# Attention steps of 20 queries in three slots instead of two, and the two weight copies of a step declared independent

## The chip, the cores and the metric

The kernel runs on one core of a Trainium2 chip. The metric is the device time of one execution in microseconds. Three runs of the kernel before took 1334.59, 1334.84 and 1337.12 us (median 1334.84).

## The reference

Three layers follow each other: an attention over 4 batches, 12 heads, 448 positions and 64 features, whose scores are mixed across heads before the softmax and whose weights are mixed across heads after it; a two-layer network with a sigmoid gate; and a mixture of 8 experts. The change touches the attention alone:

```python
scores = scale * np.matmul(q, k.transpose(0, 1, 3, 2))
scores = np.einsum('bhij,hg->bgij', scores, w_pre)
scores = scores - np.max(scores, axis=-1, keepdims=True)
attn = np.exp(scores)
attn = attn / (np.sum(attn, axis=-1, keepdims=True) + 1e-09)
attn = np.einsum('bhij,hg->bgij', attn, w_post)
return np.matmul(attn, v).astype(np.float32)
```

## The kernel before, in words

The 448 queries of a batch are cut into tiles of 120, 120, 120 and 88, so there are 16 tiles. A tile's raw scores are computed on TensorE for pairs of heads (`qk`, L89), scaled and moved out of PSUM by ScalarE and VectorE (`qk_ev`, L94 and L95), and stored to a DRAM tile `S` (L96). Tiles are cut into steps of 20 queries (the last step of an 88 tile has 8), 92 steps in all. A step's scores come back from DRAM in another layout (`relay`, L104 and L106): one partition holds one query and one head, 60 partitions hold 5 queries by 12 heads, a "unit" is 10 queries (two groups `c` of 5), and a step has two units `a` (one in the 8-query step).

For a step, `premix` (L112) mixes the heads with a block-diagonal matrix into PSUM, `maxi` (L116, VectorE) takes the negative row maximum, and `exp` (L119, ScalarE) writes the exponential E and its row sum. `weights` (L122, L123 on VectorE, L126 on GpSimd) takes the reciprocal of the sum and multiplies the second mixing matrix with it: the result is the tile M, one per unit, so that the division is part of the second mixing. `post` (L135) multiplies pieces of E with M on TensorE: 32 small matmuls per unit, whose results, already transposed, go to the PSUM tile `psa` (one buffer of two banks, one bank per group `c`, 240 columns per unit). `post_ev` copies them into the tile AT, which holds the transposed weights of a whole query tile: unit 0 by ScalarE (L142), unit 1 by VectorE (L143), each reading both banks. `av` (L151) multiplies AT with the values for two heads at a time, six times per tile, and `av_ev` (L155, L156) moves each half of a tile's result out and stores it.

The order on every engine is the order in which the program issues the instructions; no scheduler changes it. The loop over slots `s` sets it: slot s issues the relay of step s+3, Q, K and V loads, `premix`, `maxi` and `exp` of step s, `post` and `post_ev` of step s-1, the `av` calls due in this slot, the `qk` calls due (new scores for a later tile, one call per slot as a rule), `weights` of step s, and last `qk_ev`. A step thus spans two slots. All stores and loads are issued on SP in this order.

From slot 88 on, every slot also calls `beside` twice. Each call issues the next entries of the list EARLY, which belong to the second stage: loads and decodes of its packed weights (L246 on ScalarE, L251 to L254 on VectorE), splits of a float32 tile into a rounded part and a remainder (L227, L228, L259, L260 on ScalarE, VectorE and GpSimd), and the first matmuls (L268). The first of three L268 groups issued there comes in slot 92, the second in slot 93, the third in slot 95. Behind the last slot the second stage opens its remaining memory, issues two more weight loads and goes on with its own loop, in which every step decodes two weight tiles on VectorE.

The wait of VectorE's copy for ScalarE's copy comes from the framework, which orders instructions that write overlapping address ranges of one tile; the two copies of a step write interleaved columns of AT. `declare_no_dep` tells it that two instructions do not depend on each other.

Of the kernel before, what the change touches and what calls it, by code (L numbers as in the profile page):

```python
# [6 lines left out]
F32 = mybir.dt.float32  # L7
# [10 lines left out]
TI = 120  # L18
DM, FF, E = 768, 2048, 8
# [18 lines left out]
def attention(tc, qT, kT, vT, w_pre, w_post, x_out, beside=None):  # L38


    nc=tc.nc
    tiles=[(b,i0,min(TI,S-i0)) for b in range(B) for i0 in range(0,S,TI)]
    steps=[]; first={}
# [4 lines left out]
    units=lambda s: range((steps[s][2]+9)//10)  # L48
# [11 lines left out]
    def load_mix():  # L60
# [3 lines left out]
        for c in range(2):  # L64
# [2 lines left out]
            sel(out=x,in_=x,pattern=[[12,5],[0,12]],compare_op=ALU.is_ge,fill=0.0,base=11,channel_multiplier=-1)  # L67
            sel(out=y,in_=y,pattern=[[0,12],[-12,5]],compare_op=ALU.is_ge,fill=0.0,base=0,channel_multiplier=1)
            sel(out=y,in_=y,pattern=[[0,12],[12,5]],compare_op=ALU.is_ge,fill=0.0,base=11,channel_multiplier=-1)
    K={}; V={}; Q={}; St={}; G={}; PM={}; E={}; ST={}; M2={}; PA={}; AT={}; PV={}; QP={}; ready=set(); moved=set()  # L70
    def dma_k(b,p,n=2):
        t=wf.tile([128,2,S],F32,tag="K",bufs=6,name="K") if p%2==0 else K[b,p-1][1]
        for i in range(n): K[b,p+i]=(t[:,(p+i)%2],t)
        nc.sync.dma_start(out=t[:,p%2:p%2+n],in_=kT[b,2*p:2*p+2*n].rearrange("(p h) d s -> (h d) p s",h=2))
    def dma_v(b,h):
        t=w.tile([128,3,4,D],F32,tag="V",bufs=8,name="V")
        for i in range(3): V[b,h+i]=t[:,i]
        nc.sync.dma_start(out=t,in_=vT[b,:,h:h+3])
    def dma_q(t,z=None):
        b,i0,n=tiles[t]  # L80
        if t not in Q: Q[t]=wf.tile([128,6*TI],F32,tag="Q",bufs=2,name="Q")
        lo,hi=(0,6*n) if z is None else z
        nc.sync.dma_start(out=Q[t][:,lo:hi],in_=qT[b,:,6*i0+lo:6*i0+hi])
    def qk(t,p):
        b,i0,n=tiles[t]
        for z in range(2):
            r=slice(64*z,64*z+64)
            QP[t,p,z]=pq.tile([TI,S],F32,tag="q",name="psq")
            nc.tensor.matmul(QP[t,p,z][:n],Q[t][r,p*n:p*n+n],K[b,p][0][r],start=True,stop=True)  # L89
    def qk_ev(t,p):  # L90
        n=tiles[t][2]
        if p==0: St[t]=dr.tile([TI,12,S],F32,tag="S",bufs=4,name="S")
        o=wf.tile([TI,2,S],F32,tag="so",bufs=3,name="so")
        nc.scalar.activation(o[:n,0],QP.pop((t,p,0))[:n],AF.Copy,scale=0.125)  # L94
        nc.vector.tensor_scalar_mul(o[:n,1],QP.pop((t,p,1))[:n],0.125)  # L95
        nc.sync.dma_start(out=St[t][:n,2*p:2*p+2,:],in_=o[:n])  # L96
        moved.add((t,p))
    def relay(s):
        t,k,_=steps[s]
        if (t,5) not in moved: raise RuntimeError('relay before scores')  # L100
        G[s]=w.tile([124,2,S],F32,tag="G",bufs=6,name="G")
        x=St[t].rearrange("i h j -> (i h) j")
        for a in units(s):
            if qs(s,a,1)==5: nc.sync.dma_start(out=G[s][64*a:64*a+60],in_=x[12*(k+10*a):12*(k+10*a)+120].rearrange("(c p) j -> p c j",c=2))  # L104
            else:
                for c in range(2): nc.sync.dma_start(out=G[s][64*a:64*a+12*qs(s,a,c),c],in_=x[12*(k+10*a+5*c):12*(k+10*a+5*c+qs(s,a,c))])  # L106
    def premix(s):
        for a in units(s): PM[s,a]=pm.tile([128,S],F32,tag="m",name="psm")
        for a in units(s):
            for c in range(2):  # L110
                r=slice(64*a,64*a+12*qs(s,a,c))
                nc.tensor.matmul(PM[s,a][64*c:64*c+64],wp[r],G[s][r,c,:],start=True,stop=True)  # L112
        G.pop(s)
    def maxi(s,a):
        if a==0: ST[s]=w.tile([124,4,2],F32,tag="st",bufs=4,name="st")
        nc.vector.reduce_max(ST[s][:,0,a:a+1],PM[s,a][:124],axis=AX.X,negate=True)  # L116
    def exp(s,a):
        E[s,a]=w.tile([124,S],F32,tag="E",bufs=6,name="E")
        nc.scalar.activation(E[s,a],PM.pop((s,a))[:124],AF.Exp,bias=ST[s][:,0,a:a+1],scale=1.0,accum_out=ST[s][:,1,a:a+1])  # L119
    def weights(s):  # L120
        u=len(units(s)); st=ST[s]
        nc.vector.tensor_scalar_add(st[:,2,0:u],st[:,1,0:u],1e-9)  # L122
        nc.vector.reciprocal(st[:,3,0:u],st[:,2,0:u])  # L123
        for a in units(s):
            M2[s,a]=w.tile([124,60],F32,tag="M2",bufs=4,name="M2")
            nc.gpsimd.tensor_scalar_mul(M2[s,a],wq,st[:,3,a:a+1])  # L126
    def post(s,a):
        e,m=E.pop((s,a)),M2.pop((s,a))
        if a==0: PA[s]=pa.tile([128,2,512],F32,tag="a",name="psa")
        for cc in range(4):  # L130
            for cp in range(2):
                j=min(56*(2*cc+cp),S-64)
                for c in range(2):
                    r=slice(64*c,64*c+60)
                    nc.tensor.matmul(PA[s][64*cp:64*cp+64,c,240*a+60*cc:240*a+60*cc+60],e[r,j:j+64],m[r],start=True,stop=True)  # L135
    def post_ev(s,a):
        t,k,_=steps[s]
        if t not in AT: AT[t]=w.tile([128,4,12,TI],F32,tag="AT",bufs=2,name="AT")
        i=k+10*a
        o=AT[t][:,:,:,i:i+10].rearrange("p c g (r q) -> p r (c g) q",r=2)  # L140
        x=PA[s][:,:,240*a:240*a+240].rearrange("p r (m q) -> p r m q",q=5)
        if a==0: nc.scalar.copy(o,x)  # L142
        else: nc.vector.tensor_copy(o,x)  # L143
        ready.add((s,a))
    def av(t,p):
        b,i0,n=tiles[t]; l=first[t+1]-1
        if any((l,a) not in ready for a in units(l)): raise RuntimeError('values before weights')
        if p%3==0: PV[t,p//3]=pv.tile([128,3,TI],F32,tag="v",name="psv")
        ps=PV[t,p//3]
        for j in range(4):  # L150
            for z in range(2): nc.tensor.matmul(ps[64*z:64*z+64,p%3,:n],V[b,2*p+z][:,j,:],AT[t][:,j,2*p+z,:n],start=j==0,stop=j==3)  # L151
    def av_ev(t,p):
        if p%3<2: return
        b,i0,n=tiles[t]; x=w.tile([128,3,TI],F32,tag="X",bufs=3,name="X")
        nc.vector.tensor_copy(x[:,:,:n],PV.pop((t,p//3))[:,:,:n])  # L155
        nc.sync.dma_start(out=x_out[b,:,p-2:p+1,i0:i0+n],in_=x[:,:,:n])  # L156
    from collections import defaultdict
    at={k:defaultdict(list) for k in 'qakvd'}
    for t in range(NT):
        b=tiles[t][0]; n=first[t+1]-first[t]  # L160
        if t>1:
            for p in range(6): at['q'][first[t-1]-AHEAD+p*(first[t]-first[t-1])//6].append((t,p))
            at['d'][max(0,first[t-1]-AHEAD-4)].append((t,))
        m=first[t+2]-first[t+1] if t+1<NT else 3
        for p in range(6): at['a'][first[t+1]+1+p*m//6].append((t,p))
        if t%4==0 and b>0:
            for p in (0,2,4): at['k'][first[t-1]-AHEAD-9+p].append((b,p))
        if t%4==0:
            for h in (0,3,6,9): at['v'][first[t]+h//3].append((b,h))
# [4 lines left out]
    for t in range(2):  # L174
        for p in range(6): qk(t,p); qk_ev(t,p)
        if t==0:
            for s in range(LEAD): relay(s)
    for s in range(0,NS+5):
        on=s<NS
        if s+LEAD<NS: relay(s+LEAD)  # L180
        for x in at['d'][s]: dma_q(*x)
        for x in at['k'][s]: dma_k(*x)
        for x in at['v'][s]: dma_v(*x)
        if on:
            premix(s)
            for a in units(s): maxi(s,a); exp(s,a)
        if 0<=s-1<NS:
            for a in units(s-1): post(s-1,a)
            for a in units(s-1): post_ev(s-1,a)
        for x in at['a'][s]: av(*x); av_ev(*x)  # L190
        for x in at['q'][s]: qk(*x)
        if on: weights(s)
        for x in at['q'][s]: qk_ev(*x)
        if s+LEAD>=NS-1 and beside is not None:
            if front is not None: front.close(); front=None
            for _ in range(2):
                if beside is not None and beside()=="end": beside=None
# [597 lines left out]
def moe_kernel(tc, qT, kT, vT, w_pre, w_post, w_in, w_out, wg, wm, out):  # L795
    with ExitStack() as ctx:
        x=ctx.enter_context(tc.tile_pool(name="xd",bufs=1,space=bass.MemoryType.DRAM)).tile([B,128,6,S],F32,name="x_dram")
        with tc.manual_schedule():
            def rest():
                env=make_env(tc,ctx,tc.nc); env.wm=wm  # L800
                yield from moe1(tc,env,x,w_in,w_out,wg)
                yield env
            g=rest()
            attention(tc,qT,kT,vT,w_pre,w_post,x,lambda: next(g))
            env=None
            while not isinstance(env,Env): env=next(g)
            moe2(tc,env,out)
        overflow(tc,env,out)
# [48 lines left out]
```

## Time and profile before

| | |
|---|---|
| median of the runs | 1334.84 us |
| profiled execution | 1341.98 us |
| its span, first to last instruction | 1340.3 us |
| mean granted TensorE clock | 0.967 of full speed |
| TensorE busy / VectorE / ScalarE / GpSimd | 91% / 59% / 45% / 23% |
| DMA | 201.09 MB, mean 150 GB/s |

Attention fills about the first 440 us. The second stage's decode of weights follows up to about 600 us; there VectorE is busy all the time. From 600 to 1000 us TensorE is busy all the time, and the experts fill the rest. Busy time on TensorE is modelled from starts, so start-to-start distances are the safer reading; a row of the timeline merges neighbouring instructions of a line, "xN" is their number, and the bracket at its end is the idle time of that engine before it and what ended it.

### The profile page before, as it was taken

The page shows a single profiled execution, that of the slowest core. Times are in us where ns is not written, and L with a number is a line of the kernel's source. Part 1 is how long each engine was busy: PE and PEld are TensorE (multiplying, and loading weights), DVE is VectorE, ACT ScalarE, POOL GpSimd, SP SyncE. Part 2 cuts the span into 40 slices and gives each one's busy share as a digit, 9 for nine tenths or more (in the row PEclk, how much of TensorE's full clock was granted, in tenths as well). Part 3 has the DMA queues.
Part 4 walks back from the last instruction along what each step waited for, and adds up shares of the span by engine and source line. Part 5 has one row for each costly group of instructions (what it writes and reads, how often), then busy time and mean ns, then how long its engine had stood idle before and what let it go on. Part 6 is the DMA issues. An engine that isn't in the chain of part 4 may idle for free. (4 is left out here: it accounts for less than half of the span.)

```text
span 1340.3 us, 31619 instructions
## 1 busy us (share of the span) xinstructions
PE 1217.9 (91%) x13086; PEld 992.6 (74%) x13087; DVE 787.0 (59%) x1340; ACT 606.5 (45%) x1203; POOL 312.7 (23%) x385
## 2 busy tenths in 40 slices
PE   7798998898888788779999999999996979999996
PEld 2355555555555577668899899989996979999996
DVE  1565665565655799997543544454437645566663
ACT  2455555555554444434434433443334534445552
POOL 0111111111111555553121112112113202321110
PEclk9899999999999798989999999999997989999998
DMA  7887987987966355420100010000555756656500
GB/s 222 254 242 208 296 239 212 269 254 202 281 186 203 128 203 194 152 96 26 42 22 21 1 52 11 21 1 11 183 198 172 207 160 190 190 198 228 187 20 21
DMA packets 97825, 201.09 MB, mean 150 GB/s; under 512 B 29711, under 2 KB 67733, under 8 KB 97292
## 3 DMA queue, kind: packets, MB, share of 16 engines
q1 hardware_dynamic: 91596, 186.84, 45.4%
q0 software_dynamic: 6080, 12.18, 2.9%
q8 instruction: 104, 1.70, 0.5%
q14 instruction: 45, 0.37, 0.1%
HBM read 143.60 MB, written 56.43 MB: 149 GB/s over the span
## 5 line engine op out<-in xcount | busy, mean ns | idle before, releaser
L268 PE MATMUL psh<-x,ws 128*128 128x448 f32 x1152 | 264.1, 382 | 25.2 <-POOL ws L260 14.9
L268 PEld LDWEIGHTS psh<-x,ws 128*128 128x128 f32 x1152 | 224.5, 197 | 56.0 <-POOL ws L260 20.3
L285 PE MATMUL pso<-g,ws 128*128 128x448 f32 x1152 | 252.7, 369 | 0.0
L285 PEld LDWEIGHTS pso<-g,ws 128*128 128x128 f32 x1152 | 213.8, 188 | 20.1
L135 PEld LDWEIGHTS psa<-M,E 60*64 60x64 f32 x5760 | 98.2, 138 | 115.2 <-POOL M L126 103.7
L119 ACT ACTIVATE E<-psm,st 124x448 f32<-124x448 f32 x180 | 112.5, 629 | 127.3 <-DVE st L116 127.2
L126 POOL TENSOR_SCALAR M<-wq,st 124x60 f32<-124x60 f32 x180 | 78.7, 451 | 354.8 <-DVE st L123 270.1
L260 DVE TENSOR_TENSOR ws<-res,ws 128x768 fp32r<-128x768 f32 x81 | 91.4, 1128 | 105.8 <-ACT ws L259 102.8
L135 PE MATMUL psa<-M,E 60*64 60x60 f32 x5760 | 108.9, 224 | 48.7 <-POOL M L126 43.1
L278 POOL TENSOR_TENSOR g<-th,g 128x448 fp32r<-128x448 f32 x64 | 78.4, 1225 | 308.2 <-ACT g L277 308.1
L661 PE MATMUL psh<-xt,ws 128*128 128x256 f32 (+2 forms) x1152 | 147.7, 289 | 0.1
L661 PEld LDWEIGHTS psh<-xt,ws 128*128 128x128 f32 x1152 | 145.3, 190 | 0.3 <-DVE xt L653 0.3
L628 DVE TENSOR_TENSOR ws<-res,ws 128x768 fp32r<-128x768 f32 x128 | 121.9, 959 | 39.7 <-ACT ws L627 39.5
L143 DVE COPY AT<-psa 128x480 f32<-128x480 f32 x88 | 60.2, 685 | 133.1 <-ACT AT L142 133.1
L89 PE MATMUL psq<-K,Q 64*120 64x448 f32 (+1 forms) x384 | 114.8, 648 | 11.9 <-ACT so L94 7.0
L116 DVE TENSOR_REDUCE st<-psm 124x1 f32<-124x448 f32 x180 | 103.7, 617 | 14.6 <-PE psm L112 13.8
L680 PE MATMUL psy<-ws,hh 128*128 128x384 f32 x576 | 110.4, 345 | 0.0
L627 ACT CAST ws<-res 128x768 fp32r<-128x768 f32 x128 | 105.5, 832 | 7.9 <-PE psy L697 4.9
L259 ACT CAST ws<-res 128x768 fp32r<-128x768 f32 x108 | 89.9, 832 | 35.5 <-DVE res L254 35.5
L151 PE MATMUL psv<-AT,V 128*64 128x120 f32 (+1 forms) x1536 | 98.8, 273 | 6.9 <-DVE X L155 3.5
L680 PEld LDWEIGHTS psy<-ws,hh 128*128 128x128 f32 x576 | 100.9, 190 | 0.0
L112 PE MATMUL psm<-G,wp 60*64 60x448 f32 x720 | 94.5, 578 | 0.5 <-ACT E L119 0.5
(178 smaller groups left out, 1289.5 us busy)
## 6 DMA issues: line engine op xcount, KB each, us to landing
res<-in_wm SPq DMA_DIRECT2D x56, 768.0 KB
G<-S SPq DMA_DIRECT2D x176, 210.0 KB
S<-so SPq DMA_DIRECT2D x72, 420.0 KB
wd<-in_w_in SPq DMA_DIRECT2D x10, 768.0 KB
wd<-in_w_out SPq DMA_DIRECT2D x10, 768.0 KB
S<-so SPq DMA_DIRECT2D x24, 308.0 KB
V<-in_vT SPq DMA_DIRECT2D x16, 384.0 KB
K<-in_kT SPq DMA_DIRECT2D x11, 448.0 KB
```

The lines of the kernel that those rows point to most:

```text
L89: nc.tensor.matmul(QP[t,p,z][:n],Q[t][r,p*n:p*n+n],K[b,p][0][r],start=True,stop=True)
L112: nc.tensor.matmul(PM[s,a][64*c:64*c+64],wp[r],G[s][r,c,:],start=True,stop=True)
L116: nc.vector.reduce_max(ST[s][:,0,a:a+1],PM[s,a][:124],axis=AX.X,negate=True)
L119: nc.scalar.activation(E[s,a],PM.pop((s,a))[:124],AF.Exp,bias=ST[s][:,0,a:a+1],scale=1.0,accum_out=ST[s][:,1,a:a+1])
L135: nc.tensor.matmul(PA[s][64*cp:64*cp+64,c,240*a+60*cc:240*a+60*cc+60],e[r,j:j+64],m[r],start=True,stop=True)
L151: for z in range(2): nc.tensor.matmul(ps[64*z:64*z+64,p%3,:n],V[b,2*p+z][:,j,:],AT[t][:,j,2*p+z,:n],start=j==0,stop=j==3)
L268: nc.tensor.matmul(ps[:,:TB],t[:,wz,c],x[:,xz,:],start=k==0,stop=k==17); k+=1
L285: nc.tensor.matmul(OB[b][o][:,:TB],t[:,wz,c],g[:,xz,:],start=f==0 and k==0,stop=f==NF-1 and k==2)
L627: nc.scalar.copy(t[:,0,:],r[:,c])
L628: nc.vector.tensor_tensor(out=t[:,1,:],in0=r[:,c],in1=t[:,0,:].bitcast(F32),op=ALU.subtract)
L661: nc.tensor.matmul(ps,w[:,a,k*128:(k+1)*128],x[:,b,:],start=k==0 and (a,b)==(0,0),stop=k==5 and a==1)
L680: nc.tensor.matmul(PY[e][2*c+z],h[:,a,c*CP:c*CP+CP],w[:,b,z*384:z*384+384],start=f==0 and k==0,stop=f==7 and k==2)
```

## The change

`post`, `post_ev` of a step move one slot later (step s-2 in slot s), `weights` moves one slot later too (step s-1 in slot s), ahead of the slot's `av` and `qk`, and the `av` calls of a tile move one slot later. The loop has one slot more. The two copies of a step are now split by the group `c`, which is one PSUM bank each, instead of by unit: ScalarE copies group 0 of both units, VectorE group 1 of both units. In a one-unit step both engines copy half of it. All copies into one AT tile are declared independent of each other. Buffers keep their numbers.

```diff
-    def post_ev(s,a):
-        t,k,_=steps[s]
-        if t not in AT: AT[t]=w.tile([128,4,12,TI],F32,tag="AT",bufs=2,name="AT")
-        i=k+10*a
-        o=AT[t][:,:,:,i:i+10].rearrange("p c g (r q) -> p r (c g) q",r=2)
-        x=PA[s][:,:,240*a:240*a+240].rearrange("p r (m q) -> p r m q",q=5)
-        if a==0: nc.scalar.copy(o,x)
-        else: nc.vector.tensor_copy(o,x)
-        ready.add((s,a))
+    def post_ev(s,c):
+
+        t,k,n=steps[s]; u=len(units(s))
+        if t not in AT: AT[t]=w.tile([128,4,12,TI],F32,tag="AT",bufs=2,name="AT"); WA[t]=[]
+        o=AT[t][:,:,:,k:k+10*u].rearrange("p x g (a c q) -> p a c (x g) q",c=2,q=5)[:,:,c]
+        x=PA[s][:,c,0:240*u].rearrange("p (a m q) -> p a m q",a=u,q=5)
+        e=nc.scalar.copy if c==0 else nc.vector.tensor_copy
+        i=e(o[:,0],x[:,0]) if u==1 else e(o,x)
+        for j in WA[t]: tc.declare_no_dep(i.ins,j,reason="distinct queries")
+        WA[t].append(i.ins)
+        ready.add((s,c))
...
-        for p in range(6): at['a'][first[t+1]+1+p*m//6].append((t,p))
+        for p in range(6): at['a'][first[t+1]+2+p*m//6].append((t,p))
...
-    for s in range(0,NS+5):
+    for s in range(0,NS+6):
...
-        if 0<=s-1<NS:
-            for a in units(s-1): post(s-1,a)
-            for a in units(s-1): post_ev(s-1,a)
+        if 0<=s-2<NS:
+            for a in units(s-2): post(s-2,a)
+            for c in range(2): post_ev(s-2,c)
+        if 0<=s-1<NS: weights(s-1)
         for x in at['a'][s]: av(*x); av_ev(*x)
         for x in at['q'][s]: qk(*x)
-        if on: weights(s)
         for x in at['q'][s]: qk_ev(*x)
```

## Rows read from the trace of the kernel before

**Rows 1.** Waits from 50 to 400 us: who <- for whom: us, times, longest.
```profile
DVE AT L143 <- ACT AT L142: 112.6, 75, 3.3
...
PE psa L135 <- POOL M L126: 29.6, 42, 1.5
...
PE psa L135 <- issue: 5.3, 6, 1.8
```

**Rows 2.** Grouped lines of TensorE, 50 to 400 us: busy, mean ns, idle before.
```profile
L112 PE MATMUL psm<-G,wp 60*64 60x448 f32 x612 | 77.4, 567 | 0.0
```

**Rows 3.** Timeline of one slot: start us, length, engine, line, operation.
```profile
203.28 0.98 PE L112 MATMUL psm<-G,wp 60*64 60x448 f32 x8
...
204.08 1.11 PE L135 MATMUL psa<-M,E 60*64 60x60 f32 x64
...
204.37 1.16 DVE L116 TENSOR_REDUCE st<-psm 124x1 f32<-124x448 f32 x2 [0.35 <-PE psm L112]
...
205.12 1.04 PE L151 MATMUL psv<-AT,V 128*64 128x120 f32 x16
...
206.09 1.02 PE L89 MATMUL psq<-K,Q 64*120 64x448 f32 x4
...
207.04 0.98 PE L112 MATMUL psm<-G,wp 60*64 60x448 f32 x8
```

**Rows 4.** Timeline, from ScalarE's copy to the next weight matmuls.
```profile
210.64 0.64 ACT L142 COPY AT<-psa 128x480 f32<-128x480 f32 x1
...
211.31 0.69 DVE L143 COPY AT<-psa 128x480 f32<-128x480 f32 x1 [1.41 <-ACT AT L142]
211.89 0.15 DVE L122 TENSOR_SCALAR st<-st 124x2 f32<-124x2 f32 x1
...
212.07 0.17 DVE L123 RECIPROCAL st<-st 124x2 f32<-124x2 f32 x1
...
212.43 0.83 POOL L126 TENSOR_SCALAR M<-wq,st 124x60 f32<-124x60 f32 x2 [3.11 <-DVE st L123]
...
212.92 1.16 PE L135 MATMUL psa<-M,E 60*64 60x60 f32 x64
```

**Rows 5.** DMA view from 50 to 400 us: totals; queue: packets, MB, share.
```profile
DMA packets 47206, 84.56 MB, mean 242 GB/s; under 512 B 14043, under 2 KB 34671, under 8 KB 47132
...
q1 hardware_dynamic: 47132, 83.50, 82.8%
```

**Rows 6.** Windows: length, busy us of the engines, TensorE clock, DMA share, GB/s.
```profile
144.00:154.00 10.00, 9.16 (x196) 4.55 (x192) 6.35 (x17) 5.94 (x15) 1.67 (x4) 1.00 0.97 322
...
214.00:224.00 10.00, 8.97 (x205) 5.52 (x199) 5.67 (x14) 6.38 (x17) 1.67 (x4) 1.00 0.83 217
407.26:433.56 26.30, 21.88 (x634) 15.23 (x632) 14.91 (x38) 12.89 (x34) 5.84 (x14) 1.00 0.63 182
```

**Rows 7.** Timeline behind the last steps, 450 to 475 us.
```profile
450.66 1.12 PE L135 MATMUL psa<-M,E 60*64 60x60 f32 x32 [3.33 <-POOL M L126]
...
453.51 4.70 PE L268 MATMUL psh<-x,ws 128*128 128x448 f32 x18
453.62 0.53 DVE L155 COPY X<-psv 128x360 f32<-128x360 f32 x1 [3.24 <-PE psv L151]
454.07 0.55 DVE L251 TENSOR_SCALAR re<-wd 128x768 int32<-128x768 int32 x1
...
468.05 3.03 PE L151 MATMUL psv<-AT,V 128*64 128x88 f32 x48 [3.54 <-DVE X L155]
...
471.01 4.51 PE L268 MATMUL psh<-x,ws 128*128 128x448 f32 x18
471.12 0.43 DVE L155 COPY X<-psv 128x264 f32<-128x264 f32 x1 [0.87 <-PE psv L151]
```

**Rows 8.** Waits from 430 to 475 us.
```profile
DVE AT L143 <- ACT AT L142: 6.1, 4, 1.7
```

**Rows 9.** Windows behind the attention.
```profile
500.00:550.00 50.00, 39.58 (x164) 33.62 (x165) 50.00 (x42) 21.08 (x30) 29.04 (x19) 0.90 0.52 189
```

More of the change, by code (lines that the diff above doesn't have):

```diff
@@ L69, in load_mix @@
             sel(out=y,in_=y,pattern=[[0,12],[12,5]],compare_op=ALU.is_ge,fill=0.0,base=11,channel_multiplier=-1)
-    K={}; V={}; Q={}; St={}; G={}; PM={}; E={}; ST={}; M2={}; PA={}; AT={}; PV={}; QP={}; ready=set(); moved=set()
+    K={}; V={}; Q={}; St={}; G={}; PM={}; E={}; ST={}; M2={}; PA={}; AT={}; PV={}; QP={}; WA={}; ready=set(); moved=set()
     def dma_k(b,p,n=2):
@@ L135, in post @@
                     nc.tensor.matmul(PA[s][64*cp:64*cp+64,c,240*a+60*cc:240*a+60*cc+60],e[r,j:j+64],m[r],start=True,stop=True)
-    def post_ev(s,a):
-        t,k,_=steps[s]
-        if t not in AT: AT[t]=w.tile([128,4,12,TI],F32,tag="AT",bufs=2,name="AT")
-        i=k+10*a
-        o=AT[t][:,:,:,i:i+10].rearrange("p c g (r q) -> p r (c g) q",r=2)
-        x=PA[s][:,:,240*a:240*a+240].rearrange("p r (m q) -> p r m q",q=5)
-        if a==0: nc.scalar.copy(o,x)
-        else: nc.vector.tensor_copy(o,x)
-        ready.add((s,a))
+    def post_ev(s,c):
[8 more added lines that the diff above has]
+        ready.add((s,c))
     def av(t,p):
         b,i0,n=tiles[t]; l=first[t+1]-1
-        if any((l,a) not in ready for a in units(l)): raise RuntimeError('values before weights')
+        if any((l,c) not in ready for c in range(2)): raise RuntimeError('values before weights')
         if p%3==0: PV[t,p//3]=pv.tile([128,3,TI],F32,tag="v",name="psv")
```

## The prediction, made before the changed kernel was timed

> **What bounds the kernel now.** I read the page's slices first, then the waits and the grouped lines of the attention stretch, then one slot of the timeline, and last the stretch behind attention.
>
> Attention fills the first third of the span; it is a chain of 92 steps whose score mixing (L112), weight matmuls (L135), value matmuls (L151) and new scores (L89) follow each other on TensorE. Between 50 and 400 us the grouped lines count 612 L112 matmuls, eight per step [rows 2]: 76.5 slots in 350 us, 4.58 us each. In the same stretch TensorE waited 29.6 us, in 42 waits, for the tile M which GpSimd makes at L126 [rows 1]. Where it doesn't wait, the timeline shows what a slot costs: mixing at 203.28, weights 0.80 us later, values 1.04 later, scores 0.97 later, next mixing at 207.04 [rows 3]. That is 3.76 us. A slot that waits shows why [rows 4]: ScalarE copies its half of the step's weights at 210.64, VectorE's copy starts only when that has ended, at 211.31, though it needs nothing of it; the sum and reciprocal (211.89, 212.07) stand behind it on VectorE, M starts at 212.43 and the matmuls at 212.92. VectorE was held in this way 75 times, 112.6 us in all [rows 1]. So the order copy, copy, reciprocal, M is the wait that ends last.
>
> **The change, part by part.** Durations are of the profiled execution: 1341.98 us, with a span of 1340.3; the median of the runs is 1334.84, 7.1 us less. I work out a difference and take it from the median.
>
> *M a slot earlier, and the copies side by side.* The reciprocal of step s-1 no longer waits for this slot's exponentials, since those sums are a slot old. In a slot that starts at zero, the weight matmuls run from 0.80 to 1.91, the two maxima from 1.09 to 2.25 [rows 3]; VectorE's copy can then start at 2.25. From copy start to M is 1.12 us and from M to the matmuls 0.49 [rows 4], so M would let them start at 3.86, and they are wanted at 3.76 + 0.80 = 4.56. The margin is 0.7 us, and the M wait goes. What it is worth: 29.6 us as recorded, and 0.18 us more for each of the 42, because the recorded end of L112 (0.98) lies behind the start that an unhindered L135 has (0.80): 7.6. That makes 37 us in 76.5 slots, and about 38 in the 80 slots from 43 to 407 us. What is late next is TensorE's own work with its other stalls; the 5.3 us that L135 waited for nothing visible [rows 1] stay, and I allow 3 us for waits that the denser pace brings (scores, instructions, transfers). Steady gain: 35.
>
> *Slots without new scores.* From 407.26 to 433.56 seven slots take 26.3 us [rows 6]. Without L89 TensorE would need 0.80 + 1.04 + 0.97 = 2.81, but M is there only at 3.86 - 0.80 = 3.06 into the next slot's count. Seven slots of 3.06 and one more value group (0.97) make 22.4. Gain: 4.
>
> *The copies themselves* keep their size (128 x 480, two halves of 240) and cost VectorE 0.69 us as before. Four one-unit steps give VectorE an extra half copy (about 0.35 by the same row), beside TensorE: nothing. ScalarE: two exponentials, one copy, one score copy as before.
>
> *Start.* The first weights run a slot later, but at L112's next turn nothing is missing: the work moves to the end. I take 0, between +1.1 (one weight group uncovered) and -1.5 (the longest M wait [rows 1]).
>
> *The end.* The early work of the next stage (first decodes, weight splits, matmuls L268) is tied to slot numbers, and attention's last steps slide one slot past it. Every queue counts.
> (a) Around 434 to 447 VectorE waits for ScalarE's copy 4 times, 6.1 us; three of them, about 4.6 us, lie among VectorE's decodes, which set the pace there, and go [rows 8].
> (b) The last weights now stand behind the first L268 on TensorE. In the trace the last L135 (450.66) and a value group come first, L268 starts at 453.51 for 4.70 us, and VectorE's X copy at 453.62 frees the decodes at 454.07 [rows 7]. After the change: L268 to about 458.7, last weights 0.8, value group 1, VectorE's two copies 0.6; decodes at 461. Cost 7; no less than 1.4 (last weights and copies alone, if L268 has ended before VectorE comes to them), and no more than 8.
> (c) The last value groups stand behind the third L268. Now VectorE's last X copy is at 471.12, just after L151 (468.05 for 3.03), and L268 starts at 471.01 [rows 7]. After the change VectorE waits for that L268 (4.51) and two value groups (1.4 to 1.9) before it goes on: 6. Behind this VectorE is busy 50.00 of 50 us [rows 9], so both stalls are lost in full; were they hidden, it would be 0.
> On SP the two loads behind the last store slide with it and add nothing of their own. GpSimd's M of the last steps stands behind the splits as now. Sum of the end: -4.6 + 7 + 6 = +8, between -3 (only the 1.4 of (b) left) and +14 ((a) gives nothing).
>
> Total: -35 - 4 + 8 = -31. 1341.98 becomes 1311, and the median 1304.
>
> *Do the transfers allow it?* Between 50 and 400 us 84.56 MB moved at 242 GB/s, with the 16 engines taken 82.8% [rows 5]. That is 1.105 MB and 3.79 us of engine time per slot; the shortened mean slot is (350 - 37) / 76.5 = 4.09, a share of 0.93. Two stretches bound it: 322 GB/s at a share of 0.97, and 217 at 0.83, which is 261 at a full share [rows 6]. At 261 a slot can't be under 4.23. I take the mean share, so transfers don't bind, and keep the worst for a rival.
> The Trainium skill, "DMA: Bandwidth & Descriptors", section Specifications, gives about 358 GB/s of HBM per core; by an estimate from it a slot's 1.105 MB take 3.09 us, and transfers would be no limit at all. The rows differ: at 322 GB/s the share is already 0.97, so the room is smaller than the page's figure says.
>
> **The rivals.**
> *Transfers bind.* For it: the share of 0.83 to 0.97 [rows 5, 6]. Against: slots of 3.76 happen now. At the worst rate a slot is 4.23 instead of 4.58, a gain of 0.35 x 80 = 28 at most; with bursts and round trips of scores through DRAM I take half, 14: -14 - 3 + 8 = -9, 1326.
> *Only half of the change takes effect:* VectorE still waits for ScalarE. Then its copy starts, as now, 0.67 after ScalarE's [rows 4], 3.65 into a slot; M lets the matmuls start at 5.26, and the period is 5.26 + 1.04 + 0.97 + 0.95 = 8.22 for two slots, 4.11. Over normal slots that lose about 0.47 now, 0.35 is still lost: gain 10, with the ends -10 + 8 = -2, 1333. Against: the copies no longer share a PSUM half, and their dependency is declared away.
> *The end costs nothing.* If the extra slot hides under the decodes, (b) and (c) vanish: -35 - 4 - 4 = -43, 1292.
> *Slower: the end outweighs the slots.* One mechanism: VectorE's queue holds the next stage's decodes behind copies that wait for the long L268 matmuls. Its price is 13 us, up to 18 if each L268 takes half as long again as in its row. It decides where the steady part gives less than that, under 0.16 us a slot. For it: VectorE has no room behind [rows 9]. Against: 29.6 us of visible M waits [rows 1]. With a steady gain of 6 and 13 lost, 1342.
>
> **How the numbers follow.** Forecast 0.55; free end 0.13; transfers bind 0.17; half effective 0.07; slower 0.08. About 0.2% (2.7 us) is what can be told from no change. Faster: the first three and a little of the half-effective case, 0.87; same 0.05; slower 0.08. The range goes from 1288 (free end, with the 3 us of new waits saved) to 1329 (transfers bind, and 3 more).
>
> **What would show it.** Right: L135's wait for M near zero from 50 to 370 us and slots near 3.8 to 4.1; no wait of VectorE for ScalarE's copy; the first decodes starting later after their L268 than now, and a VectorE wait of some 5 us before its last X copy. Wrong: TensorE waiting for G or for scores as long as it now waits for M; or slots of 4.1 with M still late; or a VectorE without those two stalls at the end.

## The result, and the profile after

The changed kernel took 1323.97 us (median of four runs, 1320.65 to 1326.81) against 1335.98 for the kernel before in the same series: a ratio of 0.9907, 95% interval 0.9886 to 0.9928. It is faster by 12 us where 31 were forecast. The profiled execution has a span of 1325.1 us and took 1326.81, 15.2 less than the one before.

First the attention stretch. These are the waits from 50 to 400 us after the change (who, for whom, us in total, times, longest), the answer to [rows 1]:

```profile
PEld psa L135 <- POOL M L126: 18.3, 65, 0.8
DVE AT L143 <- PE psa L135: 17.7, 17, 2.0
PE psa L135 <- issue: 16.1, 13, 2.1
PE psv L153 <- issue: 7.0, 6, 2.3
```

and the grouped line that counts the slots, the answer to [rows 2] (busy, mean ns, idle before):

```profile
L112 PE MATMUL psm<-G,wp 60*64 60x448 f32 x668 | 86.6, 578 | 0.0
```

TensorE's matmuls no longer wait for M at all; only the weight load that runs ahead of them shows a rest of it. VectorE's copy waits for TensorE instead of ScalarE. 668 matmuls instead of 612 are 83.5 slots in 350 us, 4.19 us each after 4.58. But two lines that were small have grown: stalls in which TensorE waits for nothing that the profile shows ("issue") are 16.1 + 7.0 = 23.1 us. Before, L135 had 5.3 [rows 1] and the value matmuls 3.4, together 8.7:

```profile
PE psv L151 <- issue: 3.4, 4, 1.8
```

A slot without such a stall, in the timeline (start, length, engine, line):

```profile
374.52 0.98 PE L112 MATMUL psm<-G,wp 60*64 60x448 f32 x8
...
375.33 1.11 PE L135 MATMUL psa<-M,E 60*64 60x60 f32 x64
...
376.68 0.68 DVE L143 COPY AT<-psa 128x480 f32<-128x480 f32 x1
...
377.56 0.64 ACT L143 COPY AT<-psa 128x480 f32<-128x480 f32 x1
377.79 0.84 POOL L126 TENSOR_SCALAR M<-wq,st 124x60 f32<-124x60 f32 x2 [2.89 <-DVE st L123]
378.25 0.98 PE L112 MATMUL psm<-G,wp 60*64 60x448 f32 x8
```

It takes 3.73 us: VectorE copies at 376.68, before ScalarE has begun its own, and M follows at 377.79, well ahead of the weights that need it, which come after the mixing at 378.25. A slot with a stall:

```profile
349.54 0.56 PE L135 MATMUL psa<-M,E 60*64 60x60 f32 x25
352.05 0.81 PE L135 MATMUL psa<-M,E 60*64 60x60 f32 x39 [1.94 <-issue]
...
353.97 1.85 PE L89 MATMUL psq<-K,Q 64*120 64x448 f32 x4
```

The 64 matmuls of L135 break off after 25, inside the 32 of the first unit, where no data can be missing that the first 25 didn't need as well. Behind it the scores take 1.85 us instead of 1.02 [rows 3]. The windows of this place (length, busy time of TensorE, its weight loads, VectorE, ScalarE, GpSimd, then granted clock, DMA share, GB/s) show both sides of it:

```profile
349.00:353.00 4.00, 2.06 (x78) 1.47 (x72) 1.75 (x4) 1.82 (x6) 0.31 (x1) 1.00 1.00 309
353.00:357.00 4.00, 4.00 (x40) 1.82 (x40) 1.44 (x4) 1.09 (x2) 0.84 (x2) 0.57 0.57 193
```

While TensorE stood, the 16 DMA engines were taken in full; after it had stood, its granted clock was 0.57 in the mean, mostly the lower of its two levels (1.2 instead of 2.4 GHz).

Now the end, the answer to [rows 7]:

```profile
408.20 0.56 DVE L253 TENSOR_SCALAR re<-wd 128x768 int32<-128x768 int32 x1 [3.82 <-DMA wd<-in_w_in]
...
424.82 5.45 PE L270 MATMUL psh<-x,ws 128*128 128x448 f32 x18
430.20 0.69 PE L135 MATMUL psa<-M,E 60*64 60x60 f32 x32
...
430.96 0.42 DVE L143 COPY AT<-psa 128x240 f32<-128x240 f32 x1 [6.87 <-PE psa L135]
431.91 0.53 DVE L157 COPY X<-psv 128x360 f32<-128x360 f32 x1 [0.53 <-PE psv L153]
432.36 0.55 DVE L253 TENSOR_SCALAR re<-wd 128x768 int32<-128x768 int32 x1
...
448.70 5.45 PE L270 MATMUL psh<-x,ws 128*128 128x448 f32 x18
454.09 1.43 PE L153 MATMUL psv<-AT,V 128*64 128x88 f32 x32
...
455.57 0.43 DVE L157 COPY X<-psv 128x264 f32<-128x264 f32 x1 [7.70 <-PE psv L153]
...
456.68 1.02 DVE L253 TENSOR_SCALAR res<-wd 128x768 int32<-128x768 int32 x2
```

Line numbers behind L143 are two higher than before. The last weights (430.20) stand behind the first L270 group, VectorE waits 6.87 us for them, and only then goes on with decodes; the last value groups stand behind the third L270 group, and VectorE waits 7.70. A third wait is new: the first decode waits 3.82 us for its weights. Before, two copies at this place waited for ScalarE instead, and the first `res` decode came at 472.24:

```profile
434.46 0.68 DVE L143 COPY AT<-psa 128x480 f32<-128x480 f32 x1 [1.47 <-ACT AT L142]
...
440.80 0.68 DVE L143 COPY AT<-psa 128x480 f32<-128x480 f32 x1 [1.46 <-ACT AT L142]
...
472.24 2.67 DVE L251 TENSOR_SCALAR res<-wd 128x768 int32<-128x768 int32 x2
```

All traces can be cut at the same four starts: the first exponential of step 3, of step 83 (no new scores behind it) and of step 91 (the last), and the first decode into `res` (the second stage's own loop). In us:

| kernel | steps 3 to 83 | 83 to 91 | 91 to first `res` decode |
|---|---|---|---|
| before | 358.4 | 35.8 | 27.3 |
| changed | 333.5 | 32.5 | 40.4 |
| changed, again (e7) | 331.2 | 33.4 | 40.5 |
| independent only (e1) | 339.8 | 30.6 | 26.9 |
| third slot only (e2) | 347.3 | 36.4 | 40.1 |
| early work a slot later (e3) | 328.6 | 29.0 | 31.6 |
| early matmuls behind (e6) | 323.3 | 33.8 | 32.5 |
| and loads a slot earlier (e8) | 331.8 | 30.9 | 31.4 |

### The profile page after: what moved, and what is told of

Same layout as the page of the kernel before. It is cut to its first block, busy times and chain, and to the rows that moved or that the text cites. A ratio compares the mean times of both kernels' runs of the same rounds, so it can differ in the third digit from the quotient of the medians.

```text
span 1325.1 us, 31704 instructions
## 1 busy us (share of the span) xinstructions
PE 1212.9 (92%) x13086; PEld 1003.9 (76%) x13087; DVE 791.4 (60%) x1344; ACT 606.6 (46%) x1203; POOL 311.1 (23%) x385
## 5 line engine op out<-in xcount | busy, mean ns | idle before, releaser
L270 PE MATMUL psh<-x,ws 128*128 128x448 f32 x1152 | 267.4, 386 | 34.2 <-ACT ws L261 19.0
L270 PEld LDWEIGHTS psh<-x,ws 128*128 128x128 f32 x1152 | 226.8, 199 | 65.9 <-ACT ws L261 23.3
L135 PEld LDWEIGHTS psa<-M,E 60*64 60x64 f32 x5760 | 106.8, 138 | 69.9 <-issue 39.6
L262 DVE TENSOR_TENSOR ws<-res,ws 128x768 fp32r<-128x768 f32 x81 | 91.4, 1128 | 105.5 <-ACT ws L261 102.5
L630 DVE TENSOR_TENSOR ws<-res,ws 128x768 fp32r<-128x768 f32 x128 | 121.9, 959 | 40.4 <-ACT ws L629 40.3
L135 PE MATMUL psa<-M,E 60*64 60x60 f32 x5760 | 109.7, 222 | 24.2 <-issue 16.1
L95 DVE TENSOR_SCALAR so<-psq 120x448 f32<-120x448 f32 (+1 forms) x96 | 59.9, 623 | 100.3 <-PE psq L89 87.4
L629 ACT CAST ws<-res 128x768 fp32r<-128x768 f32 x128 | 105.5, 832 | 7.9 <-PE psy L699 4.9
L153 PE MATMUL psv<-AT,V 128*64 128x120 f32 (+1 forms) x1536 | 97.8, 270 | 9.9 <-issue 7.0
```

What stands on the lines that cost most here:

```text
L270: nc.tensor.matmul(ps[:,:TB],t[:,wz,c],x[:,xz,:],start=k==0,stop=k==17); k+=1
L629: nc.scalar.copy(t[:,0,:],r[:,c])
L630: nc.vector.tensor_tensor(out=t[:,1,:],in0=r[:,c],in1=t[:,0,:].bitcast(F32),op=ALU.subtract)
```

## The experiments

The chips of the later runs differ (the kernel before took 1346.20 us on that of e1 to e4 and 1337.39 on that of e5 to e8), so times are compared as ratios to the kernel before on the same chip, and stretches of the attention directly. Steps 3 to 83 of the changed kernel, e3, e6, e7 and e8 are the same program; their 323.3 to 333.5 us are the scatter of that column. For the kernel before there is one execution.

**e1: the declared independence without the third slot.** The new `post_ev`, which splits the copies by bank and declares them independent, is called in the old loop. Against the kernel before, beside the new `post_ev`:

```diff
-            for a in units(s-1): post_ev(s-1,a)
+            for c in range(2): post_ev(s-1,c)
```

> The copies split by bank and declared independent, but a step stays in two slots and nothing moves. Theory (the wait of VectorE's copy for ScalarE's is what makes M late, and the extra slot is what costs at the end): M is ready at about 4.3 us into a slot and wanted at 4.56, so between 50 and 400 us TensorE waits under 5 us for M (29.6 before, none after) and about 660 L112 matmuls run there (612 before, 668 after); the first decode no longer stands behind an L268 group, so about 25 to 29 us faster than before, ratio 0.978 to 0.982. Rival (the third slot removes the wait): M is waited for in most slots, over 15 us, 610 to 630 L112 matmuls, ratio 0.992 to 1.000.

Measured: 1324.54 us, ratio 0.9828 (0.9803 to 0.9853). The waits of TensorE for M and for nothing visible, 50 to 400 us, and the slots:

```profile
PE psa L135 <- issue: 18.0, 12, 2.8
PE psv L153 <- issue: 4.8, 4, 1.9
...
PE psa L135 <- POOL M L126: 1.7, 3, 0.6
```
```profile
L112 PE MATMUL psm<-G,wp 60*64 60x448 f32 x652 | 85.1, 577 | 0.5 <-issue 0.5
```

Without the third slot the M wait falls from 29.6 to 1.7 us. The slots are a little longer than with the third slot (339.8 against 323 to 334 us for the 80). Why they are longer isn't shown: VectorE waits 13.1 us in 39 pieces for the exponentials' sums here, but TensorE waits for M only 1.7 us, and the granted clock of this stretch is 0.98, as in the slower executions of the changed kernel. The end costs nothing (26.9 against 27.3). The gain is 22 us by the medians, 23 by the ratio, and not the 25 to 29 expected; the mechanism is the theory's, and the rival is out. The split by bank and the declaration came together here, and no run separates them.

**e2: the third slot without the independence.** The changed loop with the old `post_ev` (one unit per copy, no declaration).

> Three slots as in the changed kernel, but the copies by unit and not declared independent. Theory: VectorE's copy again starts 0.67 us after ScalarE's, M lets the matmuls start at 5.26, a slot is 4.1 us plus stalls: 620 to 640 L112 matmuls between 50 and 400 us, M waits of 15 to 30 us, gain there 10 to 15, end loses about 13: ratio 0.997 to 1.003. Rival (the third slot alone does it): 665 L112 matmuls, no M wait, ratio 0.991 as the changed kernel.

Measured: 1350.98 us, ratio 1.0036 (1.0019 to 1.0052), slightly slower and just above the range expected. The waits 50 to 400 us of VectorE and of TensorE:

```profile
DVE AT L143 <- ACT AT L142: 115.5, 78, 2.6
```
```profile
PE psa L135 <- POOL M L126: 26.3, 49, 1.4
PE psa L135 <- issue: 2.7, 2, 1.8
```

The gain in the 80 steps is 11 us and the end loses 12.8. Stalls without a visible cause are almost gone, 2.7 us, although the slots are shorter than before. TensorE waits for M in 49 places, and what the stalls wait for may arrive meanwhile; one execution can't show that.

**e3: the next stage's early work a slot later.** The edit, against the changed kernel:

```diff
-        if s+LEAD>=NS-1 and beside is not None:
+        if s+LEAD>=NS and beside is not None:
```

> The changed kernel with the calls for the next stage beginning at slot 89 instead of 88, so that attention's last steps stand to them as they did before the change. Theory (the end loses 12 to 14 us, most of it in two waits of VectorE, 6.9 and 7.7 us, behind L268 groups): both waits shrink under 4 us, the later start costs about 3 us, so 7 to 11 us faster than the changed kernel, ratio to before 0.983 to 0.986. Rival (the end is bound by something else, the loads or the decodes): no faster than the changed kernel, or 3 us slower, ratio 0.990 to 0.994.

Measured: 1321.00 us, ratio 0.9827 (0.9794 to 0.9860). VectorE's waits for attention's last results, 395 to 460 us, of the changed kernel

```profile
DVE AT L143 <- PE psa L135: 8.3, 2, 6.9
DVE X L157 <- PE psv L153: 8.2, 2, 7.7
DVE re L253 <- DMA wd<-in_w_in: 3.8, 1, 3.8
```

and of e3:

```profile
DVE X L157 <- PE psv L153: 2.6, 2, 1.4
DVE AT L143 <- PE psa L135: 1.7, 2, 1.5
DVE re L253 <- DMA wd<-in_w_in: 0.5, 1, 0.5
```

The end falls from 40.4 to 31.6 us, so 8.8 of the 13.1 us that it had lost come back. Most of what it costs is the order against the early work, not the extra slot.

**e6: only the L268 groups moved.** In EARLY, `(9,'l',(0,))` becomes `(10,'l',(0,))`, and `(14,'l',(2,))` goes to the end as `(16,'l',(2,))`; decodes and loads stay.

> The changed kernel with the first and third L268 group of the next stage issued behind attention's last weights and last value groups; decodes and loads stay at their slots. Theory (VectorE's two long waits, 6.9 and 7.7 us in the changed kernel, are waits for these groups standing ahead on TensorE): both fall under 4 us together, first decodes of slot 93 some 5 us earlier, 8 to 11 us faster than the changed kernel on the same chip, ratio to before 0.978 to 0.984. Rival (the decodes are held by loads or GpSimd anyway): within 3 us of the changed kernel.

Measured: 1315.55 us, ratio 0.9840 (0.9807 to 0.9872); the changed kernel on this chip took 1325.40. The end takes 32.5 us, and VectorE's waits for L135 and L153, 395 to 460 us, are

```profile
DVE X L157 <- PE psv L153: 5.3, 2, 3.9
...
DVE AT L143 <- PE psa L135: 3.4, 2, 1.9
```

together 8.7 instead of the "under 4" expected. So about half of the 16.5 us that the changed kernel waits there was the matmuls ahead, and of the two long waits (6.9 and 7.7, now 1.9 and 3.9) the larger part; the rest stays.

**e7: the changed kernel again.**

> The changed kernel unaltered, on the chip of these runs, for comparison. Ratio to before 0.987 to 0.993. In its profile the stalls of TensorE without a visible wait between 50 and 400 us are 18 to 26 us again, with 3 to 6 dips of the clock to half, if they belong to the kernel and not to one execution.

Measured: 1325.40 us, ratio 0.9894 (0.9859 to 0.9929). The invisible stalls, 50 to 400 us:

```profile
PE psa L135 <- issue: 19.0, 15, 2.1
PE psv L153 <- issue: 6.1, 6, 1.7
PE psq L89 <- issue: 0.8, 1, 0.8
PE psm L112 <- issue: 0.7, 2, 0.5
```

26.6 us, a little over the range expected: they belong to the kernel. The dips of the clock come and go: the mean granted clock of this stretch is 1.00 here, without a dip, and 0.98 in the first execution, which had five; e3, e6 and e8 had one, one and four. That part of the expectation missed.

**e8: e6 with the first loads a slot earlier.** `s+LEAD>=NS-2`, and 2 added to every time in EARLY.

> As the kernel with the early matmuls behind, and the next stage's first loads issued one slot earlier, its work at the same slots. Theory (VectorE's 3.8 us wait before the first decode is the weight load landing late, since slots have become shorter): that wait goes, 2 to 4 us faster than without it. Rival (the decode chain catches up behind it): within 1 us.

Measured: 1311.67 us, ratio 0.9808 (0.9774 to 0.9842), the fastest of all. The wait for the weight load is gone from VectorE's list; the medians of e6 and e8 differ by 3.9 us as the theory says, but the intervals overlap, so that size isn't settled.

**e4 and e5: fewer score reads.** About half, then about 70%, of the G loads are left out, so that a step uses the scores of an earlier one. The line in `relay`, first of e4, then of e5 (the release of G is moved to match, not shown):

```diff
+        if s%23%2==1: G[s]=G[s-1]; return
...
```
```diff
+        if s%23%4 and s%23<22: G[s]=G[s-1]; return
...
```

> The changed kernel, but every second step uses the scores of the step before it, so half of the G loads are left out. Between 50 and 400 us the changed kernel's TensorE stands 23 us with no wait that the profile shows (L135 16.1, value matmuls 7.0). Theory A (instructions reach TensorE late because their transfers share the 16 engines with the data): with a fifth of the bytes gone these stalls fall under 8 us, slots to 3.8 to 3.9 us, over 715 L112 matmuls in that stretch. Theory B (the supply of instructions is limited by itself): they stay over 16 us and the slots at 4.1 to 4.2.

> The changed kernel with three of four G loads left out (a step uses the scores of an earlier one). With half of them left out TensorE's unexplained stalls between 50 and 400 us were 12.8 us instead of 23.1 and the slots 3.95 us. Theory A (instruction transfers wait behind data on the same engines): the stalls go on falling with the bytes, to 5 to 9 us, slots 3.80 to 3.88. Theory B (part of the supply is limited by itself, by the pace of TensorE): they stay at 11 to 14 us and the slots at 3.9 to 3.95.

The stalls, 50 to 400 us, of e4 (L136 and L154 are L135 and L153 of the changed kernel)

```profile
PE psa L136 <- issue: 9.9, 10, 2.2
...
PE psv L154 <- issue: 2.9, 4, 1.2
```

and of e5:

```profile
PE psa L136 <- issue: 3.3, 6, 1.0
PE psm L113 <- issue: 1.7, 2, 1.5
PE psv L154 <- issue: 1.7, 2, 1.1
PE psq L89 <- issue: 1.3, 1, 1.3
```

with these shares of the DMA engines in the data queue, for the changed kernel, e4 and e5 (packets, MB, share):

```profile
q1 hardware_dynamic: 50221, 87.95, 85.0%
```
```profile
q1 hardware_dynamic: 40372, 73.62, 72.7%
```
```profile
q1 hardware_dynamic: 35292, 65.93, 65.9%
```

Stalls of 23.1 (26.6 in e7), 12.8 and 8.0 us at shares of 85.0, 72.7 and 65.9%; in the 80 steps alone they are 21.8 (24.5), 11.5 and 6.3. The slots got shorter at the same time (3.95 us in e4, 3.90 in e5), so TensorE asked for instructions faster and still stood less: theory A's direction twice. e4 lies between the two theories' sizes, e5 within A's for the stalls but in B's for the slots, and what lengthens its slots isn't shown. Each is one execution. Their whole times (1312.71 and 1451.75) are not read: the experts' loads follow the data, and in e5 the part for overflowing tokens ran.

**What the stalls wait for, in the single DMA packets.** The profile lists the instructions' own transfers; between 50 and 400 us of the changed kernel

```profile
q8 instruction: 61, 1.00, 1.2%
```

These are 61 packets of 16 KB for 15,361 matmuls and weight loads of TensorE, and in all ten traces there is one for 249 to 257 of them. All 161 stalls without a visible cause that the ten traces have between 50 and 400 us end 1.2 to 1.7 us behind the landing of such a packet, while the packets of the changed kernel are 5.7 us apart on average. In the changed kernel one lands at 249.55 us, and TensorE, standing since 248.65, goes on at 250.93; 268.57 and 269.89, 350.46 and 352.05 are two more. So the stalls are waits for instructions.

## Why the prediction was wrong, step by step

*Right: what was late and why.* The M wait was the wait that ended last and it went (29.6 to 0). The unhindered slot is 3.73 us (3.76 forecast). Added up over the 80 slots, the time from the start of the mixing to the start of the weight matmuls fell from 105.5 to 65.6 us (63.0 in e7): 39.9, where the prediction had 38 (its own 37 in 76.5 slots make 39 in 80). That VectorE's copy behind ScalarE's was the cause is shown by e1 and e2 together: the new copies alone remove nearly all of the wait, the third slot alone leaves 26.3 us of it. For the period under "half of the change takes effect" e2 is the test: 10 us of gain in the slots were forecast, 11 came.

*Wrong in size, and the step that failed: "I allow 3 us for waits that the denser pace brings", steady gain 35.* Measured 24.9, and 27.2 in e7. The stalls without a visible wait grew from 8.7 to 23.1 us, 14 where 3 were allowed, and they are waits for instructions. I had seen that TensorE stalled for nothing visible and wrote that these 5.3 us "stay". A wait that hides under another wait isn't in the profile: while TensorE stood for M, instructions could come in. That this is why the stalls grew is argued, not shown; the denser pace is the other reading. The first execution also had five dips of the clock where the kernel before had two. The size of the miss is uncertain: the same program gained 24.9, 27.2, 29.8, 35.1 and 26.6 us in its five executions (the changed kernel, e7, e3, e6, e8), 29 in the mean, against one execution of the kernel before. In these 80 steps its stalls were 17.1 to 24.5 us, 8 to 16 more than the 8.7 before, so the 3 was too small in every one.

*Wrong: the end, "+8", by its term (a).* (b) and (c) came as described: waits of 6.87 and 0.53 us, and of 7.70. From step 91's exponential to the first decode behind the last weights it takes 16.1 us instead of 9.2, 6.9 more; (b) said 7, but 1.7 of (a) is gone in it, so (b) itself was nearer 8.6, with an L270 group of 5.45 us instead of 4.70 and the clock at its lower level in part of it. From there to the first `res` decode it takes 24.3 instead of 18.2, 6.1 more; (c) said 6. So the end as the table cuts it lost 13.1 (40.4 against 27.3). The credit (a), -4.6, didn't show. Its waits for ScalarE went, but two of the three, 2.9 us, lie ahead of step 91's exponential, in the table's middle column, and there the first decode now waits 3.82 us for its load. I had counted loads behind the last store on SP and not the first loads, one slot ahead of their use, while slots shrank.

*Right: slots without new scores.* The seven slots went from 26.3 to 23.1 us, 23.9 in e7, for the 22.4 forecast. The rest of the middle column stayed as long as it was, with (a) gained and the load wait lost.

Sum: -24.9 - 3.3 + 13.1 = -15.1, and the profiled executions differ by 15.2; behind the first `res` decode they take as long (868.1 and 868.5 us). The forecast had -35 - 4 + 8 = -31. Of the 15.9 us between them 10 lie in the steady part; the load wait is 3.8, and what (b) took beyond its 7 is 1.6. The medians differ by 12.0, and by 12.0 again in the repeated series: the profiled execution of the kernel before lay 6.0 us above its median, that of the changed kernel 2.8.

*The rivals.* "Transfers bind" named the resource but the wrong victim: between 50 and 400 us no matmul waited for G or S, while the instructions did. Its 1326 is the nearest to the measured 1324, but by luck: its steady gain of 14 and its end of +8 (with 3 for the slots without scores, where the forecast has 4) were both too small, and cancel. "The end outweighs the slots" had the mechanism right; its price of 13 was the measured one, but the steady part stayed above it.

*What stays open.* Why the instruction packets come late. Not because they are slow themselves: the 19 ahead of a stall took 1.11 us in the median and the other 42 took 1.08, and between 600 and 950 us, where the DMA engines are taken some 15%, it is 0.95 and in e7 1.10. They start later, 6.7 us behind the packet before in the median, the others 5.1. e4 and e5 show that the stalls shrink with the data traffic. The Trainium skill, "DMA: Bandwidth & Descriptors", section Queues, rings and completion order, says that a DMA engine takes turns between the queues that have work, a packet at a time, so an instruction packet would wait for a data packet ahead of it; no run here shows that wait. A data packet takes 0.095 us on average (85.0% of 16 engines in 350 us for 50221 packets), so a single turn is short beside a stall. Whether fewer instructions per slot would end the stalls was not tried.

## What to carry to other kernels

Removing the wait that ends last uncovers those that ran beneath it. Before a forecast, look for stalls without a visible cause in the stretches where the bottleneck engine already runs unhindered, and scale them up, instead of taking their total from a trace in which another wait covers them. Even that can be too low: here 4.3 us of them stand in the 37 of 80 slots without an M wait, which makes 9 in 80 by this estimate, where 17 to 24 came. Test the two halves of a double change apart: here the independent copies (split by bank and declared) give 1.7% alone, the longer pipeline costs 0.4% alone, and the two together give 0.9 to 1.1%. And a pipeline that is one slot longer moves its last slots past whatever is tied to slot numbers; putting those matmuls and loads back in order (e8, ratio 0.9808) nearly doubled what the change brought. That is no more than e1 has without the third slot (0.9828), within the intervals, so no run here shows that the third slot is worth having.

## What the runs showed of the hardware that was not expected

Instructions share the DMA engines with data (the queue of 61 packets above), and TensorE, with all its operands at hand, stood until 1.2 to 1.7 us after a packet of its instructions had landed. With the M wait gone it stood 20 to 27 us of 350 in this way, in five executions at a data share of 85 to 87%; at 66% (e5) it stood 8. After such a stall of about 2 us the granted clock can fall (0.57 over the next 4 us) or not (1.00 in e7 with as many stalls), so that a stall's price varies from one execution to the next. The dips alone don't explain the scatter of the 80 steps: 333.5 us with five, 331.2 with none, 323.3 with one.
